# Restructuring an attention and spectral-mixing kernel: heads outermost, mode weights streamed by row group behind attention, and a hand-ordered instruction stream

## The chip, the cores and the metric

The kernel runs on one core of a Trainium2 chip. The metric is the device time of one execution in microseconds (us). Where two kernels are compared, the ratio is the mean time of one kernel's fast runs over the mean of the other's fast runs of the same rounds on the same chip, so it isn't quite the ratio of the medians that are quoted beside it. Stage times are read from one profiled execution, whose time can differ by 2 us from the median. In the profile lines PE is TensorE, PEld its weight loads, DVE VectorE, ACT ScalarE, POOL GpSimd and SP SyncE; PEclk is the TensorE clock that was granted, as a share of full speed.

## The reference, cut to what matters

```python
def _attn_ref(q, k, v, s):                     # q, k, v: 8 batches, 8 heads, 576 rows, 64 columns, fp32
    scores = scale * np.matmul(q, k.transpose(0, 1, 3, 2))
    cum = np.cumsum(np.maximum(s, 0.0), axis=-1)
    bias = -(cum[:, :, :, None] - cum[:, :, None, :])
    scores = np.where(causal, -1000000000.0, scores + np.minimum(bias, 0.0))
    # ... softmax over the last axis ...
    return np.matmul(attn, v)

def _moe_ref(x, w_r, w_i, w_ch):               # x: 8 x 576 x 512; w_r, w_i: 64 modes x 512 x 512, fp32
    X = np.fft.rfft(x, axis=1)
    Xr, Xi = (np.real(X[:, :n_modes]), np.imag(X[:, :n_modes]))
    Yr = np.einsum('bmd,mde->bme', Xr, w_r) - np.einsum('bmd,mde->bme', Xi, w_i)
    Yi = np.einsum('bmd,mde->bme', Xr, w_i) + np.einsum('bmd,mde->bme', Xi, w_r)
    # ... Y holds Yr + 1j * Yi in its first 64 modes and zeros elsewhere ...
    u = x + np.fft.irfft(Y, n=S, axis=1)
    return u + np.maximum(u @ w_ch, 0.0)
```

The mode weights are 134 MB of fp32 in memory. They need no result of attention, but each mode's product needs the transform of all 576 rows of its input columns.

## The kernel before

It runs one batch after another, eight heads in each. A weight tile there is one mode with all 512 input rows, so its product needs all heads of all batches, and the mode stage stands behind attention. Six buffers of each kind hold weights, and four modes are loaded ahead. A scheduler orders each engine's instructions over the whole program; the Python order is not the order that runs (eight z matmuls of two tiles stand in a row in its timeline below, where the Python has four).

Loads, mask and exponential of attention:

```python
        for b in range(B):
            qa = apool.tile([P, H, NT, NCHA], BF16, name="qa")
            ka = apool.tile([P, H, NT, NCHA], BF16, name="ka")
            va = apool.tile([P, H, NT, NCHA], FP16, name="va")
            for tsrc, tdst in ((q, qa), (k, ka), (v, va)):
                for T in range(NT):
                    nT = tails[T]
                    nc.gpsimd.dma_start(
                        out=tdst[:nT, :, T, :D],
                        in_=tsrc[b, :, bass.ds(T * P, nT), :].rearrange(
                            "h p d -> p h d"
                        ),
                    )
# ... cut ...
                    nJ = tails[J]
                    for (i0, i1) in chunks_for(J):
                        sc_ps = spool.tile([nJ, i1 - i0], FP32, space=bass.MemoryType.PSUM,
                                           tag="sc", name="sc_ps")
                        nc.tensor.matmul(
                            sc_ps,
                            kt_sb[:NCH, bass.ds(J * P, nJ)],
                            qt_sb[:NCH, i0:i1],
                        )
                        if i0 == J * P:
                            nc.vector.tensor_tensor(
                                out=sc_ps[:, :nJ],
                                in0=sc_ps[:, :nJ],
                                in1=negm[:nJ, :nJ],
                                op=mybir.AluOpType.add,
                            )
                        nc.scalar.activation(
                            out=p_sb[:nJ, J, i0:i1],
                            in_=sc_ps,
                            func=mybir.ActivationFunctionType.Exp,
                            bias=cumt_sb[:nJ, J, p_idx : p_idx + 1],
                            scale=0.125,
                        )
```

The mode stage and the last stage:

```python
        for mc in range(NM // MC):
            y_stage = ypool.tile([16, MC, DM], BF16, name="y_stage")
            for mi in range(MC):
                m = mc * MC + mi
                if m in pre_w:
                    wr_sb, wi_sb = pre_w.pop(m)
                else:
                    wr_sb, wi_sb = issue_w_load(m)
                yp = mpool.tile([16, DM], FP32, space=bass.MemoryType.PSUM, name="yp")
                for dt in range(DT):
                    nc.tensor.matmul(
                        yp, xt_sb[:, dt, :, :, m], wr_sb[:, dt, :],
                        start=(dt == 0), stop=False,
                    )
                for dt in range(DT):
                    nc.tensor.matmul(
                        yp, xbt_sb[:, dt, :, :, m], wi_sb[:, dt, :],
                        start=False, stop=(dt == DT - 1),
                    )
                nc.scalar.copy(out=y_stage[:, mi, :], in_=yp)
    # ... cut: results written to y_dram ...
        for b in range(B):
            yb_sb = finpool.tile([P, DM], BF16, name="yb_sb")
            nc.sync.dma_start(out=yb_sb, in_=y_dram[b].rearrange("ri m e -> (ri m) e"))
            for T in range(NT):
                nT = tails[T]
                yy_ps = finppool.tile([P, DM], FP32, space=bass.MemoryType.PSUM, name="yy_ps")
                nc.tensor.matmul(yy_ps[:nT, :], G_sb[:, T, :nT], yb_sb)
                nc.vector.tensor_tensor(
                    out=x_all[:nT, b, T, :],
                    in0=x_all[:nT, b, T, :],
                    in1=yy_ps[:nT, :],
                    op=mybir.AluOpType.add,
                )
                # ... cut: four transposes of x_all into ut_ps ...
                ut_sb = finpool.tile([P, DT, P], FP16, name="ut_sb")
                nc.vector.tensor_copy(out=ut_sb[:, :, :nT], in_=ut_ps[:, :, :nT])
                z_ps = finppool.tile([P, DM], FP32, space=bass.MemoryType.PSUM, name="z_ps")
                for dt in range(DT):
                    nc.tensor.matmul(
                        z_ps[:nT, :],
                        ut_sb[:, dt, :nT],
                        wch_sb[:, dt, :],
                        start=(dt == 0),
                        stop=(dt == DT - 1),
                    )
                o_sb = finpool.tile([P, DM], FP32, name="o_sb")
                nc.vector.scalar_tensor_tensor(
                    out=o_sb[:nT, :],
                    in0=z_ps[:nT, :],
                    scalar=0.0,
                    in1=x_all[:nT, b, T, :],
                    op0=mybir.AluOpType.max,
                    op1=mybir.AluOpType.add,
                )
                nc.sync.dma_start(out=out[b, bass.ds(T * P, nT), :], in_=o_sb[:nT, :])
```

The softmax here doesn't subtract the row's maximum and nothing guards it: scores larger than these inputs give would overflow.

## Time and profile before

| | before |
|---|---|
| time, median of 4 runs | 760.49 us (759.92 to 761.06) |
| profiled span | 757.9 us |
| attention (TensorE busy 284 of 320 us from 60 to 380 us) | to about 370 us |
| mode stage (weights at 208 GB/s) | to about 676 us |
| last stage, 40 row tiles | first addition 681.8 us, end 757.9 us |

The prediction shows how the stages are read from the strip and the windows. This is the first line of the page of the kernel before: busy us, share of the span, and the number of instructions of each engine.

```profile
PE 575.8 (76%) x2963; PEld 271.8 (36%) x2963; DVE 276.3 (36%) x980; ACT 248.8 (33%) x522; POOL 223.1 (29%) x333
```

This is the timeline of the kernel before around the start of the last stage and in its middle: start us, duration us, engine, line, operation, out<-in, count, and in brackets the idle time before it and what ended it.

```profile
681.77 1.28 DVE L347 TENSOR_TENSOR x_all<-x_all,yy_ps 128x512 f16<-128x512 f16 x2 [312.08 <-PE yy_ps L346]
...
683.59 0.69 DVE L347 TENSOR_TENSOR x_all<-x_all,yy_ps 128x512 f16<-128x512 f16 x1
...
717.04 1.99 PE L364 MATMUL z_ps<-wch_sb,ut_sb 128*64 128x512 f16 x8 [0.75 <-DVE o_sb L372]
```

VectorE adds two or three tiles before the first one is finished, and TensorE multiplies two tiles (eight matmuls) in one go. The scheduler has interleaved the tiles. The stage takes 757.9 - 681.8 = 76 us, or 1.9 us for each of 40 tiles.

### The profile page before, as it was taken

The page shows a single profiled execution, that of the slowest core. Times are in us where ns is not written, and L with a number is a line of the kernel's source. Part 1 is how long each engine was busy: PE and PEld are TensorE (multiplying, and loading weights), DVE is VectorE, ACT ScalarE, POOL GpSimd, SP SyncE. Part 2 cuts the span into 40 slices and gives each one's busy share as a digit, 9 for nine tenths or more (in the row PEclk, how much of TensorE's full clock was granted, in tenths as well). Part 3 has the DMA queues.
Part 4 walks back from the last instruction along what each step waited for, and adds up shares of the span by engine and source line. Part 5 has one row for each costly group of instructions (what it writes and reads, how often), then busy time and mean ns, then how long its engine had stood idle before and what let it go on. Part 6 is the DMA issues. An engine that isn't in the chain of part 4 may idle for free.

```text
span 757.9 us, 8398 instructions
## 1 busy us (share of the span) xinstructions
PE 575.8 (76%) x2963; PEld 271.8 (36%) x2963; DVE 276.3 (36%) x980; ACT 248.8 (33%) x522; POOL 223.1 (29%) x333
## 2 busy tenths in 40 slices
PE   3979898898989898997866666666665666649885
PEld 3645555555555555554321111111111111114442
DVE  0555665656565665655200000000000000008996
ACT  0555666656566666655211101101101101100000
POOL 7487241525243241000233222232232222100000
PEclk9999999999999999999986666666666666668999
DMA  9999694949468194000399999999999999973443
GB/s 155 166 171 132 77 58 29 64 32 64 32 41 54 9 60 27 2 1 1 52 198 208 208 207 208 208 208 208 208 208 208 208 208 208 208 124 118 154 143 128
DMA packets 189178, 94.81 MB, mean 125 GB/s; under 512 B 116496, under 2 KB 184080, under 8 KB 189136
## 3 DMA queue, kind: packets, MB, share of 16 engines
q0 software_dynamic: 180624, 81.80, 84.1%
q1 hardware_dynamic: 8512, 12.47, 4.9%
q8 instruction: 23, 0.38, 0.2%
q14 instruction: 19, 0.16, 0.1%
HBM read 165.56 MB, written 10.49 MB: 232 GB/s over the span
## 4 chain that ended last, share of the span: by engine, by line
DMA 44%; PE 20%; DVE 19%; ACT 8%; issue 6%; POOL 1%; SPq 0%; DVEq 0%; POOLq 0%
DMA wi_sb<-in_moe_w_i_dram 38%; DVE x_all L273 9%; ACT p_sb L247 8%; PE sc_ps L235 6%; DVE sc_ps L241 5%; PE av_ps L262 4%; DMA out_dram<-o_sb 3%; PE z_ps L364 3%; PE fft_ps L285 2%; DVE o_sb L372 2%; PE qt_ps L210 2%; PE kt_ps L220 1%; DMA s_sb<-in_s_dram 1%; DMA ka<-in_k_dram 1%; PE cum_psum L130 1%
## 5 line engine op out<-in xcount | busy, mean ns | idle before, releaser
L247 ACT ACTIVATE p_sb<-sc_ps,cumt_sb 128x64 f16<-128x64 f32 (+5 forms) x384 | 172.0, 480 | 113.4 <-DVE sc_ps L241 74.6
L235 PE MATMUL sc_ps<-qt_sb,kt_sb 65*128 65x512 bf16 (+5 forms) x384 | 153.6, 405 | 30.7 <-ACT p_sb L247 27.2
L325 PE MATMUL yp<-wi_sb,xbt_sb 128*16 128x512 bf16 x256 | 108.7, 574 | 61.5 <-DMA wi_sb<-in_moe_w_i_dram 61.5
L347 DVE TENSOR_TENSOR x_all<-x_all,yy_ps 128x512 f16<-128x512 f16 (+1 forms) x40 | 25.5, 675 | 312.1 <-PE yy_ps L346 312.1
L241 DVE TENSOR_TENSOR sc_ps<-sc_ps,negm 128x128 f32<-128x128 f32 (+1 forms) x320 | 88.9, 283 | 120.3 <-PE sc_ps L235 116.9
L320 PE MATMUL yp<-wr_sb,xt_sb 128*16 128x512 bf16 x256 | 91.9, 496 | 47.7 <-DMA wr_sb<-in_moe_w_r_dram 47.1
L329 ACT CAST y_stage<-yp 16x512 bf16<-16x512 f32 x64 | 36.7, 574 | 272.1 <-PE yp L325 272.1
L262 PE MATMUL av_ps<-va,p_sb 128*128 128x65 f16 (+1 forms) x960 | 113.6, 245 | 4.6 <-ACT p_sb L247 2.8
L262 PEld LDWEIGHTS <-p_sb 128*128 128x128 f16 (+1 forms) x960 | 78.8, 126 | 89.8 <-issue 42.4
L273 DVE TENSOR_SCALAR x_all<-av_ps,rcp_sb 128x64 f16<-128x64 f32 x320 | 88.1, 343 | 2.1
L229 POOL MEMSET p_sb<- 128x320 f16 x64 | 23.8, 372 | 207.1 <-PE av_ps L262 207.1
L158 POOL DMA_DIRECT2D wr_sb<-in_moe_w_r_dram x64 | 47.7, 745 | 121.6 <-DMA wr_sb<-in_moe_w_r_dram 91.9
L325 PEld LDWEIGHTS <-xbt_sb 128*16 128x16 bf16 x256 | 31.9, 125 | 130.3 <-issue 124.4
L161 POOL DMA_DIRECT2D wi_sb<-in_moe_w_i_dram x64 | 47.6, 743 | 95.0 <-DMA wi_sb<-in_moe_w_i_dram 93.2
L320 PEld LDWEIGHTS <-xt_sb 128*16 128x16 bf16 x256 | 24.7, 117 | 120.1 <-DMA wr_sb<-in_moe_w_r_dram 93.3
L220 PE MATMUL kt_ps<-ident,ka 128*65 128x128 bf16 (+1 forms) x320 | 64.0, 303 | 1.8 <-POOL ka L187 1.6
L235 PEld LDWEIGHTS <-kt_sb 65*128 65x128 bf16 (+1 forms) x384 | 47.1, 124 | 19.0 <-issue 6.2
L210 PE MATMUL qt_ps<-ident,qa 128*65 128x128 bf16 (+1 forms) x320 | 52.2, 298 | 1.2 <-DVE qa L199 0.8
L220 PEld LDWEIGHTS <-ka 128*65 128x65 bf16 (+1 forms) x320 | 38.7, 157 | 29.7 <-issue 21.4
L364 PE MATMUL z_ps<-wch_sb,ut_sb 128*128 128x512 f16 (+1 forms) x160 | 40.7, 387 | 8.9 <-DVE o_sb L372 8.2
L226 ACT COPY kt_sb<-kt_ps 65x576 bf16<-65x576 bf16 x64 | 39.8, 622 | 12.8 <-PE kt_ps L220 9.5
L210 PEld LDWEIGHTS <-qa 128*65 128x65 bf16 (+1 forms) x320 | 36.6, 161 | 14.4 <-issue 13.0
(40 smaller groups left out, 325.5 us busy)
## 6 DMA issues: line engine op xcount, KB each, us to landing
wr_sb<-in_moe_w_r_dram POOLq DMA_DIRECT2D x64, 512.0 KB, 20.0
wi_sb<-in_moe_w_i_dram POOLq DMA_DIRECT2D x64, 512.0 KB, 20.0
out_dram<-o_sb SPq DMA_DIRECT2D x32, 256.0 KB, 2.1
qa<-in_q_dram POOLq DMA_DIRECT2D x32, 128.0 KB, 5.5
ka<-in_k_dram POOLq DMA_DIRECT2D x32, 128.0 KB, 4.8
va<-in_v_dram POOLq DMA_DIRECT2D x32, 128.0 KB, 5.4
y_scratch<-y_stage SPq DMA_DIRECT2D x16, 64.0 KB, 4.3
yb_sb<-y_scratch SPq DMA_DIRECT2D x8, 128.0 KB, 2.0
```

What stands on the lines that cost most here:

```text
L158: nc.gpsimd.dma_start(out=wr_sb, in_=moe_w_r[m].rearrange("(dt p) e -> p dt e", p=P))
L161: nc.gpsimd.dma_start(out=wi_sb, in_=moe_w_i[m].rearrange("(dt p) e -> p dt e", p=P))
L210: nc.tensor.transpose(qt_ps[:NCH, bass.ds(T * P, nT)], qa[:nT, h, T, :NCH], ident16[:nT, :nT],)
L220: nc.tensor.transpose(kt_ps[:NCH, bass.ds(T * P, nT)], ka[:nT, h, T, :NCH], ident16[:nT, :nT],)
L235: nc.tensor.matmul(sc_ps, kt_sb[:NCH, bass.ds(J * P, nJ)], qt_sb[:NCH, i0:i1],)
L241: nc.vector.tensor_tensor(out=sc_ps[:, :nJ], in0=sc_ps[:, :nJ], in1=negm[:nJ, :nJ], op=mybir.AluOpType.add,)
L247: nc.scalar.activation(out=p_sb[:nJ, J, i0:i1], in_=sc_ps, func=mybir.ActivationFunctionType.Exp, bias=cumt_sb[:nJ, J, p_idx : p_idx + 1], ...
L262: nc.tensor.matmul(av_ps[:wI, I, :], p_sb[:nJ, J, bass.ds(I * P, wI)], va[:nJ, h, J, :NCH], start=(i_av == 0), stop=(i_av == n_av - 1),)
L273: nc.vector.tensor_scalar(out=x_all[:, b, I, h * D : (h + 1) * D], in0=av_ps[:, I, :D], scalar1=rcp_sb[:, I : I + 1], scalar2=av_ps[:, NT ...
L320: nc.tensor.matmul(yp, xt_sb[:, dt, :, :, m], wr_sb[:, dt, :], start=(dt == 0), stop=False,)
L325: nc.tensor.matmul(yp, xbt_sb[:, dt, :, :, m], wi_sb[:, dt, :], start=False, stop=(dt == DT - 1),)
L364: nc.tensor.matmul(z_ps[:nT, :], ut_sb[:, dt, :nT], wch_sb[:, dt, :], start=(dt == 0), stop=(dt == DT - 1),)
```

## The change

The intent is to let the weights stream while attention runs. Heads become the outer loop, in four groups of two heads, with the eight batches inside: 32 iterations. Two heads are 128 input columns. Once a group is done for all batches, the weight rows that belong to these columns can be multiplied, while the next group's attention runs. A weight tile is now four modes with 128 input rows, 18 buffers hold them, and the sum over the four row groups lies in SBUF in fp32. A mode matmul fills only 32 of the 128 output partitions, so four of them are put side by side in the array (column tiles). The mask is added on TensorE, the division is one operation for each head. The scheduler is switched off; the order is written by hand. The core of the diff, with cuts:

```diff
@@ order and loads
+    ctx.enter_context(tc.manual_schedule())
-            for tsrc, tdst in ((q, qa), (k, ka), (v, va)):
-                for T in range(NT):
-                    nT = tails[T]
-                    nc.gpsimd.dma_start(
-                        out=tdst[:nT, :, T, :D],
-                        in_=tsrc[b, :, bass.ds(T * P, nT), :].rearrange(
-                            "h p d -> p h d"
-                        ),
-                    )
+    def load_qkv(n):
+        if n >= N:
+            return
+        g, b = divmod(n, B)
+        q2 = qkpool.tile([P, NT, 2, D], BF16, name="q2", tag="q2")
+        k2 = qkpool.tile([P, NT, 2, D], BF16, name="k2", tag="k2")
+        hs = slice(2 * g, 2 * g + 2)
+        for src, dst in ((q, q2), (k, k2), (v, v2[n % NV])):
+            for h in range(2):
+                nc.gpsimd.dma_start(
+                    out=dst[:, : NT - 1, h, :D],
+                    in_=src[b, 2 * g + h, : (NT - 1) * P, :].rearrange("(T p) d -> p T d", p=P),
+                )
+            nc.gpsimd.dma_start(
+                out=dst[:NL, NT - 1, :, :D],
+                in_=src[b, hs, (NT - 1) * P :, :].rearrange("h p d -> p h d"),
+            )
+        loaded[n] = (q2, k2)
+
...
+    def load_w(upto):
+        nonlocal w_issued
+        while w_issued < min(upto, len(wq)):
+            g, c, ri = wq[w_issued]
+            t = wpool.tile([P, WM, DM], BF16, name="w_sb", tag="w")
+            src = (moe_w_r, moe_w_i)[ri]
+            nc.gpsimd.dma_start(
+                out=t,
+                in_=src[c * WM : (c + 1) * WM, g * P : (g + 1) * P, :].rearrange("m p e -> p m e"),
+            )
+            wt[(g, c, ri)] = t
+            w_issued += 1
@@ mask on TensorE, division in one operation
-                        if i0 == J * P:
-                            nc.vector.tensor_tensor(
-                                out=sc_ps[:, :nJ],
-                                in0=sc_ps[:, :nJ],
-                                in1=negm[:nJ, :nJ],
-                                op=mybir.AluOpType.add,
-                            )
...
-                nc.vector.reciprocal(out=rcp_sb, in_=av_ps[:, :, D])
-                for I in range(NT):
-                    nc.vector.tensor_scalar(
-                        out=x_all[:, b, I, h * D : (h + 1) * D],
-                        in0=av_ps[:, I, :D],
-                        scalar1=rcp_sb[:, I : I + 1],
-                        scalar2=av_ps[:, NT - 1, D : D + 1],
-                        op0=mybir.AluOpType.mult,
-                        op1=mybir.AluOpType.bypass,
-                    )
+            ps = scpool.tile([P, 512], FP32, name="sc_ps", tag="sc")
+            first = True
+            for J, i0, w, c0 in bank:
+                if i0 == J * P:
+                    nJ = tails[J]
+                    nc.tensor.matmul(
+                        ps[:nJ, c0 : c0 + nJ], ident16[:nJ, :nJ], negm[:nJ, :nJ],
+                        start=first, stop=False, skip_group_check=True,
+                    )
+                    first = False
...
+        nc.vector.reciprocal(out=rcp, in_=ps[:, :, D])
+        c0 = (2 * g + h) * D
+        nc.vector.tensor_tensor(
+            out=x_all[:, b, :, c0 : c0 + D],
+            in0=ps[:, :, :D],
+            in1=rcp.unsqueeze(2).to_broadcast([P, NT, D]),
+            op=ALU.mult,
+        )
@@ modes by row group, in column tiles
-                for dt in range(DT):
-                    nc.tensor.matmul(
-                        yp, xt_sb[:, dt, :, :, m], wr_sb[:, dt, :],
-                        start=(dt == 0), stop=False,
-                    )
-                for dt in range(DT):
-                    nc.tensor.matmul(
-                        yp, xbt_sb[:, dt, :, :, m], wi_sb[:, dt, :],
-                        start=False, stop=(dt == DT - 1),
-                    )
-                nc.scalar.copy(out=y_stage[:, mi, :], in_=yp)
+    def modes(g, c):
+
+        ps = auxpool.tile([P, DM], FP32, name="yp", tag="aux")
+        for x in range(4):
+            par, ri = divmod(x, 2)
+            for cg in range(4):
+                m = c * MC + 2 * cg + par
+                xs = (xs_r, xs_i)[ri][g % 2]
+                nc.tensor.matmul(
+                    ps[32 * cg : 32 * cg + 32, :],
+                    xs[:, m, :],
+                    wt[(g, m // WM, ri)][:, m % WM, :],
+                    start=(x == 0), stop=(x == 3),
+                    tile_position=(0, 32 * cg), skip_group_check=True,
+                )
+        if g == 0:
+            nc.vector.tensor_copy(out=y_acc[:, c, :], in_=ps)
+        elif g < NG - 1:
+            nc.vector.tensor_tensor(out=y_acc[:, c, :], in0=ps, in1=y_acc[:, c, :], op=ALU.add)
+        else:
+            yb = spool.tile([P, DM], BF16, name="y_bf", tag="y_bf")
+            nc.vector.tensor_tensor(out=yb, in0=ps, in1=y_acc[:, c, :], op=ALU.add)
+            nc.sync.dma_start(out=y_dram[c], in_=yb)
@@ the main loop
+        for n in range(N):
+            if n + LA < N:
+                load_qkv(n + LA)
+
+            if n < B:
+                load_w(min(WB, 4 * (n + 1)))
+            else:
+                load_w(WB + 4 * (n - B))
+            cum_rows(n + 1)
+            scores(n, 0)
+            transposes(n + 1, 0)
+            av(n - 1, 1)
+            scores(n, 1)
+            fft(n - 1)
+            transposes(n + 1, 1)
+            av(n, 0)
+            if n > B:
+                modes((n - 1) // B - 1, (n - 1) % B)
+            if n == N // 2:
+                nc.gpsimd.dma_start(out=wch_sb, in_=moe_w_ch.rearrange("(dt p) e -> p dt e", p=P))
+                nc.gpsimd.dma_start(out=G_sb, in_=d_G.rearrange("c (T p) -> c T p", p=P))
+        av(N - 1, 1)
+        fft(N - 1)
+        modes(NG - 2, NCK - 1)
+        load_w(len(wq))
+        for c in range(NCK):
+            modes(NG - 1, c)
+
@@ the last stage: the same statements, copy on ScalarE, no scheduler
         for b in range(B):
             yb_sb = finpool.tile([P, DM], BF16, name="yb_sb")
             for ri in range(2):
                 nc.sync.dma_start(out=yb_sb[64 * ri : 64 * ri + 64, :], in_=y_rows[b, ri])
             for T in range(NT):
                 nT = tails[T]
                 yy_ps = finppool.tile([P, DM], FP32, name="yy_ps")
-                nc.vector.tensor_copy(out=ut_sb[:, :, :nT], in_=ut_ps[:, :, :nT])
+                nc.scalar.copy(out=ut_sb[:, :, :nT], in_=ut_ps[:, :, :nT])
```

## The prediction

> **What bounds the kernel now.** I read the 40-slice strip of the page first, to split the span into stages, and checked the split with the busy time of each engine by window.
>
> ```profile
> PE   3979898898989898997866666666665666649885
> PEclk9999999999999999999986666666666666668999
> DMA  9999694949468194000399999999999999973443
> GB/s 155 166 171 132 77 58 29 64 32 64 32 41 54 9 60 27 2 1 1 52 198 208 208 207 208 208 208 208 208 208 208 208 208 208 208 124 118 154 143 128
> ```
>
> A slice is 18.95 us. There are three stages. Attention fills slices 1 to 19, to about 370 us: TensorE is nearly full and the transfer engines are idle in its second half. The mode stage runs to about 676 us: the transfer engines sit at 208 GB/s without a gap. The last stage (inverse transform, residual, channel matmul) takes the rest. The windows answer gives the same with numbers:
>
> ```profile
> 60.00:380.00 320.00, 283.97 (x1867) 163.44 (x1865) 189.74 (x757) 190.81 (x413) 104.00 (x167) 1.00 0.58 43
> 380.00:670.00 290.00, 183.83 (x464) 51.08 (x462) 0.00 (x0) 33.30 (x58) 79.66 (x108) 0.67 1.24 208
> 680.00:758.00 78.00, 62.62 (x360) 28.09 (x360) 62.61 (x120) 0.00 (x0) 0.00 (x0) 0.94 0.39 135
> ```
>
> The columns are the window, its length, then busy us of PE, PEld, DVE, ACT and POOL, the granted clock, a DMA share that can pass 1, and GB/s written. In the mode stage VectorE does nothing at all, and attention moves only 43 GB/s: the two stages use different resources and stand end to end. The chain of work that ended last names who holds the span:
>
> ```profile
> DMA wi_sb<-in_moe_w_i_dram 38%; DVE x_all L273 9%; ACT p_sb L247 8%; PE sc_ps L235 6%; DVE sc_ps L241 5%; PE av_ps L262 4%; DMA out_dram<-o_sb 3%; PE z_ps L364 3%; PE fft_ps L285 2%; DVE o_sb L372 2%; PE qt_ps L210 2%; PE kt_ps L220 1%; DMA s_sb<-in_s_dram 1%; DMA ka<-in_k_dram 1%; PE cum_psum L130 1%
> ```
>
> The weight transfer alone is 38%. Attention is a ring in which no engine is the sole bound: TensorE score, VectorE mask (L241), ScalarE exponential, TensorE product, VectorE normalisation (L273).
>
> [...]weight rows of 2 KB move at 208 GB/s written, q, k and v rows of 256 B alone at 153 to 154 (window from 14 us).[...]208 GB/s of bf16 written is 416 GB/s of fp32 read, and I use the measurement.[...]
>
> ```profile
> 14.00:16.00 2.00, 2.00 (x11) 2.00 (x11) 0.00 (x0) 0.00 (x0) 2.00 (x3) 1.00 2.55 153
> 16.00:18.00 2.00, 2.00 (x12) 2.00 (x11) 0.00 (x0) 0.00 (x0) 2.00 (x5) 1.00 2.47 154
> ```
>
> **The change, part one: transfers.** All bytes stay. Weights are 128 loads of 512 KB as written; at 208 GB/s one takes 2.52 us, together 323 us. The q, k and v data are 14.16 MB as written; at 154 GB/s that is 92 us. The channel weights and the inverse matrix add about 4. So 419 us of transfers must pass before the last mode matmul, against about 370 + 305 now. Overlap is the gain; the transfer engines become the only bound of the first two stages if compute stays below them.
>
> **Part two: compute of one iteration** (one batch, two heads; 32 of them). Now a head takes 4.89 us, the spacing of the L273 entries in the chain (208.84 to 213.73), and a batch 42.6, so two heads with their share of the transform take 10.6.
> ScalarE keeps its six exponentials a head, 681 + 633 + 525 + 421 + 312 + 305 ns by the groups by shape, or 5.75 us for two; the k copy of 622 ns leaves it.
> VectorE loses ten mask additions (298 ns, 224 for the small one) and ten normalisations of 343 ns, and gets four copies of 441, two normalisations of about 500, two reciprocals of 186, four small transform copies of about 280, and one sum of about 680: near 4.9 us.
> TensorE: the timeline shows back-to-back transposes of full 128 columns at about 55 ns, products at 55 to 85, 512 columns at 215. Ten transposes instead of twenty, ten added mask matmuls, scores of 3,200 columns, 30 products, five transform matmuls and sixteen mode matmuls, four abreast, give 0.6 + 0.6 + 1.5 + 2.1 + 0.4 + 1.1 = 6.3 us; without concurrency of the column tiles, 8.7. In program order with waits, I take 8 us an iteration. The transfers of a full iteration are 2.9 (q, k, v) + 10.1 (four weight tiles) = 13.0 us. So from the ninth iteration on compute waits for transfers, and the compute savings are mostly hidden.
>
> **Part three: what keeps the transfers from running all the time.** GpSimd issues all of them, about 745 ns each[...]:
>
> ```profile
> L158 POOL DMA_DIRECT2D wr_sb<-in_moe_w_r_dram x64 | 47.7, 745 | 121.6 <-DMA wr_sb<-in_moe_w_r_dram 91.9 <-PE yp L320 26.3 <-issue 3.2
> ```
>
> The new q, k, v loads are 9 small ones an iteration, 6.4 us to issue for 2.9 us of data. The built order shows that every issue waits for the one eight before it, that about 15 us of memsets stand among the first loads, and that weights start only after four groups: near 42 us. By then 12 us of data have moved. Next come 18 weight tiles and four groups (57 us), to about 102. The 18 buffers are then full, and the nineteenth tile is issued only after the first mode sum in iteration 9, behind five more groups that issue in 32 us: to about 127. From there: 20 iterations of 13.0, three of weights alone at 10.1, 18 last tiles (45) and the 4: 339, to 466. Between groups I allow a bubble of 1 to 1.5 us, since small loads fill the window of eight while weights could run: about 25. Last weight at about 492.
>
> **Part four: the last stage.** The scheduler is switched off, and the built order of the new kernel has, for each of 40 row tiles, one matmul, addition, four transposes, copy, four matmuls, output operation, and only then the next tile. The kernel before interleaves two tiles (pairs of z groups, x8, in its timeline) and is VectorE bound: 1.9 us a tile.
>
> ```profile
> L372 DVE SCALAR_TENSOR_TENSOR o_sb<-z_ps,x_all 128x512 f32<-128x512 f32 (+1 forms) x37 | 25.2, 681 | 4.9 <-DMA out_dram<-o_sb 4.5 <-PE ut_ps L355 0.2
> L347 DVE TENSOR_TENSOR x_all<-x_all,yy_ps 128x512 f16<-128x512 f16 (+1 forms) x35 | 22.3, 674 | 0.0
> L361 DVE COPY ut_sb<-ut_ps 128x512 f16<-128x512 f16 (+1 forms) x37 | 14.3, 388 | 3.6 <-PE ut_ps L355 2.6
> ```
>
> The copy moves to ScalarE (0.57 us, as its 512-wide copies now take), which takes load off VectorE but the tiles now run in series: 0.68 addition + 0.39 transposes + 0.57 copy + 1.03 four matmuls + 0.68 output + five handovers of 0.06 = 3.65 us; only the next first matmul hides. Thirty-two full tiles at 3.65 and eight half tiles at 3.3 are 143; some lowered clock adds perhaps 7: 150, against 77 now. This is a loss of about 73 us inside the gain.
>
> **Sum.** 492 + about 9 from last weight to first addition (mode matmuls, sum, write and read back: 1.88 + 0.58 + 1.88 + 2.02 in the chain now) + 150 + 3 for the last store = 654. Rounded down a little because the bubbles may be smaller: 648.
>
> **The rivals.** (a) The transfers pack better than I think, no bubbles and a quicker start: last weight at 465, total 620. For it: they hold 208 GB/s when eight large loads are queued. Against it: two in three issues are now small. (b) In-order TensorE becomes the bound at 14 us or more an iteration, from single buffers of the transposes and products: last weight at 530, total 690. For it: nothing can fill a wait any more. Against it: the sums are 6 to 9 us and the order was arranged by hand. (c) The last stage costs less, 3.2 us a tile, or the clock falls to 0.67 there as in the mode stage and it costs 4.2: total 630 or 670. (d) Everything hidden and the last stage as before: 570. The built order speaks against it.
>
> **Range and chances.** The spread is about 20 us from transfers, 15 from the last stage and a tail from (b): 605 to 690. Even (b) with a slow last stage stays below 745, so faster by over 2% is nearly sure, 0.97; within 2% 0.02; slower 0.01.
>
> **What would show it.** Right: no separate mode stage; the transfer share near full from about 130 to 490 us; TensorE waits on weight tiles; a last stage of 140 to 165 us in which the chain passes addition, transposes, copy, z matmuls and output in every tile at 3.5 to 4 us. Wrong: an iteration above 13 us while transfers are idle, a mode group of sixteen above 2 us mattering to the end, a last stage below 120 us, or a last weight before 450.

The sum: 492 + 9 + 150 + 3 = 654. Three of its terms are my allowances, worked out from no trace: the mode matmuls four abreast (1.1 us for sixteen; 1.05 was measured after), the bubble of 1 to 1.5 us and the 7 us for a lowered clock. That every issue waits for the load eight before it shows in the traces. In the mode stage of the kernel before, where a load takes 2.52 us, each lands 20.0 us (median) after its issue. In the kernel after, the weight tiles issued from 203.40 to 205.63 us landed at 209.17, 211.78, 214.27 and 216.95, and the loads eight places after them were issued at 209.46, 212.07, 214.55 and 217.24; none of GpSimd's 418 loads starts with more than seven others out. The "in-order" of rival (b) shows there too: TensorE stood idle for 7.12 us ahead of the q transposes at 202.75 us and then did the fifteen products behind them, which use no q, without a wait. Within a mode group it does not show (e5).

## The result, and the profile after

| | before | after | predicted for after |
|---|---|---|---|
| time, median of 4 runs | 760.49 us | 759.3 us (757.31 to 761.38) | 648 us |
| ratio, 95% interval | | 0.999 (0.9967 to 1.0014) | |
| last weight landed | about 676 us | about 536 us | 492 us |
| first addition of the last stage | 681.8 us | 544.4 us | 501 us |
| last stage to the end | 76 us | 215 us | 153 us |

The change moved nothing: the ratio lies within 2% of one, and the predicted 648 us and the range up to 690 were both missed. The table says at once that this is no change without effect. The last stage starts 137 us earlier and takes 139 us longer. That these two cancel is a coincidence of two sizes.

The page of the kernel after: its first line, then four rows of the 40-slice strip (a slice is 19 us).

```profile
PE 402.5 (53%) x3015; PEld 201.2 (26%) x3021; DVE 215.2 (28%) x504; ACT 171.6 (23%) x425; POOL 313.2 (41%) x454
...
PE   3544548845654466665566664222355546455445
...
PEclk9975858966777656576565767555555555555555
DMA  7699999999999999999999999999211111111111
GB/s 68 40 151 145 176 150 68 126 167 153 166 176 172 169 156 163 151 169 175 150 155 150 171 180 209 211 211 209 65 52 46 41 55 55 41 43 55 47 50 49
```

TensorE lost 173 us of busy time and, but for the stretch from 120 to 140 us, no stage has it full any more. The transfer engines are busy up to slice 28 and nearly idle from slice 29 on; in these last eleven slices the granted clock is 5 tenths. Busy doesn't mean fast: in slice 7 they move 68 GB/s at the same 9 tenths. The windows of the kernel after (columns as in the prediction) give the stages:

```profile
40.00:120.00 80.00, 40.68 (x366) 25.91 (x365) 23.23 (x64) 26.39 (x70) 49.48 (x71) 0.64 1.25 150
120.00:140.00 20.00, 19.40 (x243) 12.74 (x246) 14.74 (x42) 14.21 (x38) 20.00 (x30) 0.98 1.13 73
160.00:440.00 280.00, 158.73 (x1466) 93.36 (x1465) 87.70 (x230) 82.69 (x214) 164.67 (x231) 0.68 1.29 164
460.00:536.00 76.00, 19.29 (x134) 3.84 (x123) 6.43 (x12) 0.00 (x0) 16.29 (x22) 0.54 1.22 208
544.00:757.00 213.00, 115.02 (x354) 36.33 (x359) 52.02 (x80) 21.73 (x40) 0.00 (x0) 0.50 0.14 48
```

From 160 to 440 us weights and q, k and v share the engines at 164 GB/s, short of the 208 that weights alone reach from 460 us. From 120 to 140 us only q, k and v move, at 73 GB/s; GpSimd (20.00 of 20) does nothing but issue them, and TensorE is full too (19.40). In the last stage TensorE is busy 115 of 213 us at half clock, and no engine is full.

The groups of the kernel after, two costly ones: busy us, mean ns of one, then idle time before and what ended most of it.

```profile
L218 PE MATMUL tr_ps<-ident,q 128*128 128x128 bf16 (+1 forms) x160 | 23.0, 276 | 175.1 <-DMA q<-in_q_dram 167.2
L402 PE MATMUL z_ps<-wch_sb,ut_sb 128*128 128x512 f16 (+1 forms) x160 | 75.7, 629 | 27.5 <-ACT ut_sb L399 27.5
```

A z matmul has 629 ns where it had 387 before. TensorE waited 167 us for q tiles. The waits of the kernel after (us in total, times, longest us), with the two issue waits of GpSimd and one that I had not thought of, the read-back of the mode sums:

```profile
PE tr_ps L218 <- DMA q<-in_q_dram: 167.2, 23, 10.3
...
POOL k L127 <- DMA w_sb<-in_moe_w_i_dram: 44.8, 23, 2.8
...
POOL v L123 <- DMA w_sb<-in_moe_w_r_dram: 40.7, 20, 2.8
...
PE yy_ps L389 <- DMA yb_sb<-y_scratch: 36.5, 8, 5.7
```

One iteration of the middle on TensorE, from the timeline of the kernel after:

```profile
202.75 0.75 PE L218 MATMUL tr_ps<-ident,q 128*128 128x128 bf16 x5 [7.12 <-DMA q<-in_q_dram]
...
208.29 0.40 PE L325 MATMUL yp<-w_sb,xs_r 128*32 128x512 bf16 x4
208.51 0.39 PE L325 MATMUL yp<-w_sb,xs_i 128*32 128x512 bf16 x4
208.73 0.39 PE L325 MATMUL yp<-w_sb,xs_r 128*32 128x512 bf16 x4
208.95 0.39 PE L325 MATMUL yp<-w_sb,xs_i 128*32 128x512 bf16 x4
...
217.75 0.77 PE L218 MATMUL tr_ps<-ident,q 128*128 128x128 bf16 x5 [7.12 <-DMA q<-in_q_dram]
```

The next iteration starts 15.0 us later, of which TensorE waited 7.1 for q. This one is on the short side: from 142.15 to 442.51 us such starts are 15.8 us apart in the mean (19 iterations). Sixteen mode matmuls pass in 1.05 us, four at a time. The end of the modes and one full tile of the last stage, from the same timeline:

```profile
538.06 0.69 DVE L338 TENSOR_TENSOR y_bf<-yp,y_acc 128x512 bf16<-128x512 f32 x1 [9.90 <-PE yp L325]
544.42 0.69 DVE L390 TENSOR_TENSOR x_all<-x_all,yy_ps 128x512 f16<-128x512 f16 x1 [5.67 <-PE yy_ps L389]
...
580.70 0.68 DVE L390 TENSOR_TENSOR x_all<-x_all,yy_ps 128x512 f16<-128x512 f16 x1
...
581.43 0.61 PE L395 MATMUL ut_ps<-ident16h,x_all 128*128 128x128 f16 x4 [1.38 <-DVE x_all L390]
582.13 0.59 ACT L399 COPY ut_sb<-ut_ps 128x512 f16<-128x512 f16 x1 [4.02 <-PE ut_ps L395]
...
582.77 1.89 PE L402 MATMUL z_ps<-wch_sb,ut_sb 128*128 128x512 f16 x4 [0.73 <-ACT ut_sb L399]
...
584.70 0.69 DVE L407 SCALAR_TENSOR_TENSOR o_sb<-z_ps,x_all 128x512 f32<-128x512 f32 x1 [3.32 <-PE z_ps L402]
585.31 0.68 DVE L390 TENSOR_TENSOR x_all<-x_all,yy_ps 128x512 f16<-128x512 f16 x1
```

The step from one addition to the next is 4.61 us, and the five parts follow one another; only the next tile's first matmul runs beside the end of the z matmuls and the output operation. Where a batch ends, more is added:

```profile
593.50 0.68 DVE L407 SCALAR_TENSOR_TENSOR o_sb<-z_ps,x_all 64x512 f32<-64x512 f32 x1 [2.92 <-PE z_ps L402]
...
594.81 1.19 SPq L385 DMA_DIRECT2D yb_sb<-y_scratch  x2
597.81 0.10 PEld L389 LDWEIGHTS <-G_sb 128*128 128x128 bf16 x1 [5.23 <-DMA yb_sb<-y_scratch]
597.82 0.61 PE L389 MATMUL yy_ps<-yb_sb,G_sb 128*128 128x512 bf16 x1 [4.35 <-DMA yb_sb<-y_scratch]
```

The read-back for the next batch is written behind the last output store of this batch. That store waits for `o_sb`, the read-back leaves behind it at 594.81, and TensorE gets its data at 597.8. Seven such boundaries hold 36.5 - 5.7 = 31 us (the first of the eight waits, of 5.7 us, lies before the first addition).

### The profile page after: what moved, and what is told of

It reads as the page before. It is cut to its first block, busy times and chain, and to the rows that moved or that the text cites. A ratio compares the mean times of both kernels' runs of the same rounds, so it can differ in the third digit from the quotient of the medians.

```text
span 759.6 us, 8258 instructions
## 1 busy us (share of the span) xinstructions
PE 402.5 (53%) x3015; PEld 201.2 (26%) x3021; DVE 215.2 (28%) x504; ACT 171.6 (23%) x425; POOL 313.2 (41%) x454
## 5 line engine op out<-in xcount | busy, mean ns | idle before, releaser
L261 ACT ACTIVATE p_sb<-sc_ps,cumt_sb 128x512 f16<-128x512 f32 (+5 forms) x384 | 148.6, 486 | 297.5 <-PE sc_ps L252 237.1
L218 PE MATMUL tr_ps<-ident,q 128*128 128x128 bf16 (+1 forms) x160 | 23.0, 276 | 175.1 <-DMA q<-in_q_dram 167.2
L123 POOL DMA_DIRECT2D v<-in_v_dram x64 | 49.6, 792 | 88.8 <-DMA w_sb<-in_moe_w_r_dram 40.7
L245 PE MATMUL sc_ps<-negm,ident 128*128 128x128 bf16 (+1 forms) x320 | 71.2, 259 | 0.0
L279 PE MATMUL av_ps<-v,p_sb 128*128 128x65 f16 (+1 forms) x960 | 60.5, 221 | 5.9 <-POOL p_sb L175 5.5
L147 POOL DMA_DIRECT2D w_sb<-in_moe_w_r_dram x64 | 50.5, 789 | 26.6 <-DMA w_sb<-in_moe_w_r_dram 20.4
L252 PE MATMUL sc_ps<-qtB,ktB 128*128 128x512 bf16 (+2 forms) x192 | 60.3, 396 | 0.0
L147 POOL DMA_DIRECT2D w_sb<-in_moe_w_i_dram x64 | 50.3, 786 | 21.7 <-DMA w_sb<-in_moe_w_i_dram 17.8
L123 POOL DMA_DIRECT2D k<-in_k_dram x64 | 51.7, 833 | 18.3 <-DMA w_sb<-in_moe_w_r_dram 15.1
L123 POOL DMA_DIRECT2D q<-in_q_dram x64 | 50.3, 828 | 2.3 <-issue 1.5
L252 PE MATMUL sc_ps<-qtA,ktA 65*128 65x512 bf16 (+2 forms) x192 | 44.7, 312 | 3.0 <-DVE ktA L223 3.0
```

The source lines that it names most:

```text
L123: nc.gpsimd.dma_start(out=dst[:, : NT - 1, h, :D], in_=src[b, 2 * g + h, : (NT - 1) * P, :].rearrange("(T p) d -> p T d", p=P),)
L147: nc.gpsimd.dma_start(out=t, in_=src[c * WM : (c + 1) * WM, g * P : (g + 1) * P, :].rearrange("m p e -> p m e"),)
L218: nc.tensor.transpose(ps[:, bass.ds(T * P, nT)], src[:nT, T, :, :].rearrange("p h d -> p (h d)"), ident16[:nT, :nT],)
L245: nc.tensor.matmul(ps[:nJ, c0 : c0 + nJ], ident16[:nJ, :nJ], negm[:nJ, :nJ], start=first, stop=False, skip_group_check=True,)
L252: nc.tensor.matmul(ps[:nJ, c0 : c0 + w], kt[:, bass.ds(J * P, nJ)], qt[:, i0 : i0 + w], start=False, stop=(x == len(bank) - 1), skip_group ...
L261: nc.scalar.activation(out=pt[:nJ, o : o + w], in_=ps[:nJ, c0 : c0 + w], func=ACTF.Exp, bias=cumt_sb[:nJ, J, pidx : pidx + 1], scale=0.125,)
```

## The experiments

Ten kernels were run, each an edit of the kernel after. Beside them the kernel before was run, not the kernel after; the two agree within 0.4% (0.9967 to 1.0014). All gave the right result except the one that is marked. The theory at the start: the overlap works, the last stage loses its gain to three causes (tiles in series, half clock, late read-back), and the stream is slowed by the order of small and large loads. The rivals: TensorE in order, above all the mode matmuls, sets the iteration; or the last stage costs more for a reason other than its order.

| run | time, us (runs) | before beside it | ratio, 95% interval |
|---|---|---|---|
| e1 read-back early | 724.29 (2) | 758.63 | 0.9546 (0.9489 to 0.9602) |
| e2 e1 + idle matmuls | 690.3 (2) | 758.63 | 0.9098 (0.904 to 0.9155) |
| e3 tiles interleaved by hand | 611.01 (2) | 758.63 | 0.8053 (0.8008 to 0.8097) |
| e4 loads mixed | 716.07 (2) | 758.63 | 0.9437 (0.9374 to 0.95) |
| e5 mode loops swapped | 755.91 (2) | 757.8 | 0.9973 (0.9947 to 0.9999) |
| e6 few weights (wrong result) | 512.57 (2) | 757.8 | 0.6763 (0.6738 to 0.6787) |
| e7 e3 + e4 | 565.56 (2) | 757.8 | 0.7462 (0.7442 to 0.7482) |
| e8 e7 + weights from the start | 549.58 (4) | 757.8 | 0.7257 (0.7228 to 0.7286) |
| e9 twelve matmuls added | 754.84 (4) | 757.56 | 0.9969 (0.9949 to 0.9988) |
| e10 scheduler on for the last stage | 616.49 (4) | 757.56 | 0.8137 (0.8125 to 0.8149) |

### e1: the read-back a batch ahead

```diff
...
+        yb_next = load_yb(0)
         for b in range(B):
-            yb_sb = finpool.tile([P, DM], BF16, name="yb_sb")
-            for ri in range(2):
-                nc.sync.dma_start(out=yb_sb[64 * ri : 64 * ri + 64, :], in_=y_rows[b, ri])
+            yb_sb = yb_next
+            if b + 1 < B:
+                yb_next = load_yb(b + 1)
```

> Only the read-back of the mode sums (yb_sb) for the next batch is issued one batch earlier, so that it no longer stands behind the last output store of the batch before on SyncE's queue. Theory A (the queue order makes TensorE wait at each batch boundary): seven of the eight waits of yy_ps on yb_sb (36.5 us in all, 5.7 of it the first) go, so about 30 us less: 729. Rival (the read-back itself is slow or waits for the writes of the sums): less than 10 us gained, 750 or more.

The waits view of e1 has one such wait left, the one ahead of the first addition, and the window over its last stage still shows the clock at 0.50:

```profile
PE yy_ps L396 <- DMA yb_sb<-y_scratch: 5.7, 1, 5.7
```

```profile
550.00:718.00 168.00, 106.90 (x330) 33.63 (x333) 47.73 (x75) 19.98 (x37) 0.00 (x0) 0.50 0.16 57
```

The time fell by 34 us against the kernel before, and the early read-back is the whole of this edit. In the profiled runs the last stage went from 215 to 184 us, which is the 31 us of the waits; the other 3 are not explained by the edit.

### e2: matmuls that only keep TensorE busy

The edit of e1, and `filler(6)` after the yy matmul, `filler(3)` after the transposes of every tile:

```diff
+        def filler(k):
+            for _ in range(k):
+                nc.tensor.matmul(dum, ident16h, wch_sb[:, 0, :])
```

> As the run with the early read-back, and TensorE does matmuls into a bank that nobody reads where it would wait in the last stage: 3 of 512 columns after the transposes, 6 after the first matmul of a tile. The order of all useful work stays. Theory B (the last stage is a series of handovers, and 0.96 us of its 4.61 a tile is the clock of 0.5): granted clock near 1.0 in the stage, four z matmuls 1.0 to 1.1 us instead of 1.89, a tile 3.6 to 3.8 us, so 32 to 38 us below the run with the early read-back: about 693. Rival (the clock does not depend on how busy TensorE is there, or the handovers bound the tile): clock stays 0.5 and the fillers lengthen the tile by 1 us or more, 760 and above.

The timeline of e2 in one tile, and the window over its last stage:

```profile
601.58 0.68 DVE L405 TENSOR_TENSOR x_all<-x_all,yy_ps 128x512 f16<-128x512 f16 x1
...
603.44 1.04 PE L418 MATMUL z_ps<-wch_sb,ut_sb 128*128 128x512 f16 x4
...
604.53 1.46 PE L387 MATMUL dum<-wch_sb,ident16h 128*128 128x512 f16 x6
...
605.12 0.68 DVE L405 TENSOR_TENSOR x_all<-x_all,yy_ps 128x512 f16<-128x512 f16 x1
```

```profile
560.00:680.00 120.00, 117.25 (x594) 47.05 (x599) 42.49 (x67) 18.47 (x34) 0.00 (x0) 1.00 0.21 74
```

TensorE does useless work in its gaps (busy 117 of 120 us, 107 of 168 in e1), the clock is granted in full (1.00, 0.50 in e1), four z matmuls take 1.04 us in place of 1.89, and the program is 34 us shorter than e1. From one addition to the next (601.58 to 605.12 us) the step is 3.54 us. So the lowered clock cost about 34 us, and it came from TensorE's idle share. The tiles still run in series.

### e3: the last stage interleaved by hand

```diff
+        load_yb(0)
+        front(0); front(1); middle(0)
+        for i in range(NTL):
+            front(i + 2)       # yy matmul and addition; read-back of the next batch
+            middle(i + 1)      # four transposes and the copy
+            # four z matmuls, o_sb and the store of tile i, as before
```

> The last stage alone, reordered by hand: first matmul and addition two tiles ahead, transposes and copy one tile ahead of the four z matmuls, and the read-back a batch ahead. Same operations and counts. Theory C (program order with each tile in series is what makes the last stage 216 us, against 77 in the kernel before): a tile 1.5 to 1.9 us, last stage 65 to 85 us with a clock near 1.0, in all 610 to 630. Rival (the stage is bound by an engine or the clock whatever the order): more than 3 us a tile, 690 or more.

The window over the last stage of e3:

```profile
540.00:605.00 65.00, 59.49 (x354) 26.68 (x358) 49.97 (x79) 21.70 (x40) 0.00 (x0) 0.95 0.44 153
```

The stage runs from 540.4 to 609.6 us, 69 us, with TensorE busy 59 of 65 us at a clock of 0.95. The program is 148 us shorter than the kernel after. All three causes go together here. Beyond e2, another 79 us came from taking the tiles out of series. Arithmetic and bytes are those of the kernel after.

### e4: small loads between large ones

```diff
+            if between is not None:      # in load_qkv, after the loads of q, of k and of v
+                between()
...
-                load_qkv(n + LA)
-            ...
+                load_qkv(n + LA, between=lambda: load_w(min(upto, w_issued + 1)))
+            load_w(upto)
```

> Only the order of the loads on GpSimd's queue in the loop: the four weight tiles of an iteration are issued between the loads of q, k and v (after q, after k, after v, and one more) instead of after all nine. Same loads and bytes. Theory D (at most eight loads are outstanding, and nine small ones in a row empty the queue of the transfer engines while GpSimd still issues): the period of an iteration falls from 15.0 to 13 or 13.5 us, last weight tile near 495 instead of 536, in all about 718. Rival (the 256-byte rows slow the transfer engines by themselves, or GpSimd's issue time is the bound): period unchanged, 750 or more.

The eight outstanding loads are those measured in the kernel after, beside the prediction.

The window of e4 over the middle:

```profile
160.00:440.00 280.00, 170.82 (x1609) 98.30 (x1611) 94.72 (x248) 85.28 (x222) 174.00 (x242) 0.70 1.41 185
```

The same loads, with one weight tile after q, one after k and two after v in place of nine small loads in a row, move at 185 GB/s in place of 164. (In e4 the last q, k and v are out at 403 us, and weights go alone after that; from 160 to 400 us it is 182.) The last mode sum came at 494.3 us in place of 538.1, and the time fell by 43 us. So order alone held these transfers back. The iteration did not become as short as expected: over the same 19 iterations it is 14.1 us in the mean (13 or 13.5 was expected) where the kernel after has 15.8, and 10 of the 43 us were won before them.

### e5: the two mode loops swapped (inconclusive)

```diff
-        for x in range(4):
-            par, ri = divmod(x, 2)
-            for cg in range(4):
+        for cg in range(4):
+            for x in range(4):
+                par, ri = divmod(x, 2)
```

> Only the two loops of the mode matmuls are swapped, so that the four matmuls of one column group stand next to each other: same instructions, same sums, but no four neighbours that could run side by side. Theory E (TensorE's work in an iteration is hidden behind the loads, 7 us of idle time an iteration): a group of sixteen takes about 3.5 us instead of 1.05, and the time stays at 757 to 762, at most 8 us more (the one group after the last weight tile, and slower modes of the last eight groups). Rival (TensorE's time counts in every iteration): 23 iterations times 2.4 us, about 55 us more, 815.

This was to put the four matmuls of one column tile in a row (with xs_r, xs_i, xs_r, xs_i), so that the tiles could not run beside one another. (The 3.5 us expected for a group is an estimate: sixteen times the 0.215 us of a 512-column matmul.) It didn't do that. One group of sixteen in the timeline of e5 for TensorE:

```profile
132.99 0.43 PE L325 MATMUL yp<-w_sb,xs_r 128*32 128x512 bf16 x4
133.22 0.42 PE L325 MATMUL yp<-w_sb,xs_i 128*32 128x512 bf16 x4
133.43 0.42 PE L325 MATMUL yp<-w_sb,xs_r 128*32 128x512 bf16 x4
133.65 0.42 PE L325 MATMUL yp<-w_sb,xs_i 128*32 128x512 bf16 x4
```

Four products with xs_r start within about 0.05 us of one another (0.43 us for the four, 0.39 for one), although in the program a product with xs_i stands between any two of them, and a tile has only two with xs_r. How this comes about is not shown. (Built once more, e5 has its matmuls in the order of the program, tile after tile.) The group takes 1.08 us, as in the kernel after. The mode groups did not get slower, so the run doesn't say whether slower ones would matter. Run e9 asks that in another way.

### e6: weights loaded once only (wrong result)

```diff
-        while w_issued < min(upto, len(wq)):
+        while w_issued < min(upto, WB):
...
-                    wt[(g, m // WM, ri)][:, m % WM, :],
+                    wt[wq[(2 * (m // WM) + ri) % 16]][:, m % WM, :],
```

> Wrong result on purpose: only the first 18 of the 128 weight tiles are loaded, and all mode groups read the first sixteen. Everything else as in the changed kernel. Theory F (from iteration 9 on the loads set the pace, and the compute of the change is far quicker): iterations of 6.3 to 7 us once the 18 tiles are in, attention over near 265 us, last mode group near 275, last stage 216 us as before: 490 to 510. Rival (compute or GpSimd's issues hold an iteration at 10 us or more): 570 and above.

Only 18 of the 128 weight tiles are loaded, and every mode group reads the first sixteen again (relative error 0.03). The window of e6:

```profile
140.00:160.00 20.00, 20.00 (x258) 12.50 (x255) 15.50 (x42) 14.63 (x39) 20.00 (x30) 1.00 1.13 73
```

An iteration takes 6.4 us (mode groups at 136.43, 142.84 and 149.24 us in the timeline), and TensorE works without a pause (20.00 of 20, no waits): its own work is the bound then, close to the 6.3 us that the prediction had summed. GpSimd is close behind: it issues without a pause too, nine loads in 6.28 us (q at 136.20 and 142.48). The time is a little above the 490 to 510 that were expected. The last mode sum comes at 290.8 us, 247 us earlier than in the kernel after. The last stage stays what it was: its first addition starts at 297.1 us and the span ends at 512.1, 215 us. The weight stream holds the first two stages, and nothing in the last stage comes from it.

### e7: e3 and e4 together

> Both repairs together: weight loads issued between those of q, k and v, and the last stage reordered. Theories C and D speak of different stretches, so their gains of 148 and 42 us add: 565 to 575. Rival (the last stage or the loads had a cause in common, such as the lowered clock): more than 590.

565.56 us. The two gains of 148 and 43 us from 759 would make 568: they add. The two problems are independent.

### e8: weights from the first microseconds

The edits of e7, the start memsets on VectorE, and weight tiles among the first q, k and v loads:

```diff
...
+    load_w(1)                               # after load_qkv(0)
+    load_qkv(1, between=early_w(3))
+    load_qkv(2, between=early_w(5))
-        nc.gpsimd.memset(qtB[i][0:64, :], 0.0)
+        nc.vector.memset(qtB[i][0:64, :], 0.0)   # and all the other start memsets
-            upto = min(WB, 4 * (n + 1)) if n < B else WB + 4 * (n - B)
+            upto = min(WB, 5 + 2 * (n + 1)) if n < B else WB + 4 * (n - B)
```

> As the run with both repairs, and the start is changed: the first weight load stands right after the first q, k, v group, two weight tiles go with each group until the 18 buffers are full, and the memsets move from GpSimd to VectorE. Theory G (until 140 us the transfer engines are idle about half of the time because GpSimd has memsets and small loads to issue before it reaches weights): the first reuse of a weight buffer comes near 100 us instead of near 125, so 25 to 45 us less than the run before it: 525 to 545. Rival (the loads of the start compete with q, k and v, and attention starts later by as much): less than 10 us gained.

549.58 us, with a correct result: the best of all, 208 us below the kernel before. The last mode sum came at 471.7 us, 18 earlier than in e7. The gain of 16 us is below what I expected. "Idle about half of the time" was not to be seen in the page of the kernel after: over its first seven slices (133 us) the transfer engines are busy 6 to 9 tenths and move 40 to 176 GB/s. The strip of e8 still has a slice at 72 GB/s near 100 us: all 18 buffers are full then, and q, k and v go alone until the first buffer comes free at 107.7 us. How the gain divides between the early weights and the moved memsets was not tested.

### e9: twelve more matmuls in every mode group

```diff
+        for _ in range(12):
+            nc.tensor.matmul(ps, ident16, wt[(g, (c * MC) // WM, 0)][:, 0, :], skip_group_check=True)
```

> The loop swap did not lengthen the mode groups, so TensorE's work is added directly: twelve matmuls of 512 columns into the bank of each mode group, ahead of the group, whose first matmuls clear it (result stays right). At full clock that is 12 times 0.215 = 2.6 us in each of 32 groups. Theory E (TensorE's work in an iteration is hidden behind the loads): 23 of the groups lie in idle time, only the last group or two add 3 to 8 us: 760 to 766. Rival (it counts in every iteration): 60 to 83 us more, 815 to 840.

The timeline and the waits of e9:

```profile
301.82 2.76 PE L321 MATMUL yp<-w_sb,ident 128*128 128x512 bf16 x12
```

```profile
PE tr_ps L218 <- DMA q<-in_q_dram: 103.6, 23, 9.4
```

The added matmuls take 2.76 us of an iteration, and the result stays right, so nothing of them is left in the bank. The time did not rise (754.84 against 757.56 of the kernel before beside it). The wait for q fell from 167.2 to 103.6 us: 63.6 us, which is 23 times 2.76. The added work went into the wait, one for one. This refutes the rival that TensorE sets the iteration.

### e10: the scheduler on for the last stage alone

```diff
-    ctx.enter_context(tc.manual_schedule())
+    manual = ExitStack()
+    manual.enter_context(tc.manual_schedule())
...
+    manual.close()      # ahead of the last stage
```

> The manual schedule ends before the last stage, so the scheduler orders that stage as it did in the kernel before; all instructions up to the last mode group stand as in the changed kernel, and no operation is added or removed. Theory C (it is the order that costs): the last stage falls from 216 us to 70 to 90, clock 0.9 or more, in all 612 to 635. Rival (what counts is the copy moved to ScalarE or the read-back in two pieces): 700 or more.

The built order of e10 is that of the kernel after up to the last mode group. The window over its last stage:

```profile
535.00:612.00 77.00, 63.97 (x360) 28.81 (x360) 50.70 (x80) 21.51 (x40) 0.00 (x0) 0.93 0.39 137
```

The source of the last stage is unchanged, and the stage takes 76 us (first addition 537.9, end 613.7), as in the kernel before. So nothing but the order of the instructions made it 215 us: neither the ScalarE copy nor the read-back in another layout. The hand-written interleaving of e3 is 7 us shorter.

## Why the prediction was wrong, point by point

- **Part one, transfers: right.** Weights alone move at 208 to 211 GB/s, and the loads are the bound of the first two stages (e6, e9).
- **Part two, compute: right.** An iteration runs from 202.75 to about 210.6 us, its start at a lowered clock (0.50 to 206 us, 1.00 from 206.5): 7.9 us where the prediction took 8, and is hidden. At full clock it takes 6.4 us (e6) where the sum was 6.3. A mode group takes 1.05 us where 1.1 was predicted.
- **Part three, what keeps the transfers from running: mechanism right, sizes off.** The term "a bubble of 1 to 1.5 us" measured about 2.8: an iteration is 15.8 us in the mean and not 13.0 plus 1.25. Read 1 us at a time, the rate falls to between 42 and 107 GB/s from 202 to 206 us, when the last eight loads that were issued are all small. From the first reuse of a buffer at 141.5 to the last q, k and v group at 442.7 us, 19 iterations took 301 us: some 50 us of bubbles in place of 25 (the channel weights and the inverse matrix, about 4, are taken off). The step "to about 127" came at 141.5. The five groups before it took 35 us, near the 32 of the sum, but they began at 106.6 only, since the iterations before them had the bubble already (14.8 to 17.5 us). Together the last weight landed 44 us late: 14 from the late reuse, some 25 from the bubbles, the rest behind the last group. e4 shows that order makes the bubble (164 GB/s with nine small loads in a row, 182 with large ones between, both from 160 to 400 us); GpSimd's issue time does not separate the two (0.79 to 0.83 us for 64 KB, 0.79 for 512 KB, means of the kernel after). The waits of GpSimd's small loads for weight tiles fit the reason given in the prediction, that nine small loads in a row fill the eight places: the ninth to twelfth load from 203.40 us on each begin 0.28 to 0.29 us after the landing of the tile eight before. TensorE did wait for loads, but for q (167 us), more than for the weight tiles that the prediction named (57 us). "The transfer share near full" came true and told nothing, since it is nearly as high at 73 GB/s (1.13) as at 208 (1.22).
- **Part four, the last stage: the step that failed most.** It was right that the tiles run in series, and the sum of 3.65 us a tile is close to what e2 measured at full clock (3.54); the handovers of the tile shown above are 0.04 to 0.09 us where I took 0.06. It failed in "some lowered clock adds perhaps 7". The clock was 0.50 throughout, four z matmuls took 1.89 us and not 1.03, and the step was 4.61: 40 tiles of 0.96 more make 38 us, 31 above the allowance, and e2 measured 34. And it left out the read-back at the batch boundaries altogether: 31 us in the waits, 34 in e1. The two make up the miss of the stage, 215 against 153.
- **The sum.** The first addition came 43 us late and the stage was 62 us longer: 105 us over the 654 of the sum, which gives the 759 measured. I had rounded 654 down to 648.
- **The rivals.** (a), better packing, is refuted by the period of 15.8 us. (b), TensorE as the bound, is refuted by e9, although the last weight came where (b) had put it, at 536 against 530: the number agreed for a wrong reason. (c), a slow clock in the last stage, was the right idea with too small a step: it stopped at 4.2 us and a clock of 0.67, a value carried over from another stage. (d) has its last stage come true only with the scheduler or a hand interleaving (e3, e10).
- **Sums and readings.** 42 and 57 make 99 and not "about 102", and of the "20 iterations" one had its q, k and v counted already among the "five more groups"; both are about 3 us. The transfer engines of the kernel before are idle only in slices 17 to 19, not in all of attention's second half. That its last stage "is VectorE bound" does not hold up in e10: VectorE's busy time falls from 62.6 to 50.7 us and the stage stays at 76. What bounds it is not shown.
- **The range.** I let three errors vary one at a time and took 745 us as the limit. All of them fell on the same side, and the one that I hadn't seen came on top.

**What stays open.** e5 left unanswered how much the column tiles gain over one-at-a-time matmuls: sixteen took 1.05 us, and sixteen at the 0.23 us of e9's twelve would take 3.7, an estimate of 3.5 times that no run tested. At what busy share the clock comes back isn't settled: it stayed at 0.50 with TensorE busy 64% (e1, 107 of 168 us) and was 0.93 at 83% (e10), but a busy share itself depends on the clock (four z matmuls are 1.89 us at 0.50 and 1.04 at 1.00). Nor is it settled how long the gaps must be: in the mode stage of the kernel before TensorE is never idle for more than 2.0 us at a time and the clock is 0.67, and in e1's last stage, from the first addition on, its longest wait is 1.4 us and the clock stays at 0.50. What keeps e4's iteration at 14.1 us, above the 13.0 of its transfers, is not shown. How the 148 us of e3 divide between order and clock is only bounded by e1 and e2, which take the causes away in one sequence.

## What to carry to other kernels

When a scheduler is switched off, read the built order of every stage that it used to arrange, not only of the stage that is being rebuilt: here a last stage with nearly unchanged source (e10 clears the two changes) went from 76 to 215 us and gave back a gain of 137. The chain in series cost twice here, since it also left TensorE so idle (busy 115 of 213 us) that the clock stayed at 0.50, and filling the gaps brought 1.00 (e2); so a step of such a chain should be worked out at the lowered clock too, and every load in it should be looked up in its issuing engine's order. Try small loads between large ones rather than in a row: here the order alone was worth 43 us.
